# Routing groups, the pace of the second stage and the order of the tail in a fused attention and adapter kernel

## The chip, the core and the metric

The kernel runs on one core of a Trainium2 chip. The metric is the device time of one launch in microseconds, the median of three runs. One more execution was recorded by the hardware profiler; all rows below come from it. The engines are PE (TensorE, with PEld for its weight loads), DVE (VectorE), ACT (ScalarE), POOL (GpSimd) and SP, which here only issues DMAs. Each engine works through its own queue in order.

## The reference

Four batches of 12288 queries of 128 channels attend to a pooled key/value map, and the result runs through a mixture of rank-16 adapters, two out of eight per token.

```python
kv_pool = kv.reshape(B, H // 4, 4, W // 4, 4, C).mean(axis=(2, 4))    # 768 keys per batch
kv_flat = kv_pool.reshape(B, -1, C) @ w_sr                            # keys and values are one
a = softmax(q @ kv_flat.T / sqrt(C))
x = (a @ kv_flat).reshape(B * N, 128)
logits = x @ w_gate                                                   # 8 experts
w = softmax over the two largest logits, 0 elsewhere
out = x + sum over e of w[:, e] * (x @ A[e]) @ B[e]
```

## The kernel before

**Tiling.** The 49152 tokens are 96 chunks of 512 tokens (T), each as S = 4 sub-tiles of 128; NB = 24 chunks make a batch. The gate's logits come with the attention: `vx` holds, for each key, 128 value channels, 8 columns of value times w_gate, and a one, so that `acc` has 137 columns, the last being the softmax's denominator.

**First stage of a chunk.** `scores(k, r)`, r = 0..2: PE writes two 128x512 products into one of two `sg` buffers (pool ps_s) and ACT takes the exponential into `em`. `attend(k, s)`: PE sums 6 products of 137 columns for each sub-tile into `acc`, of which there is one buffer (ps_a). `normalize(k)`: DVE takes a reciprocal (L258) and one product of 128x544 (L263), which frees `acc`. `top(k)`: DVE sorts the 8 logits of each sub-tile (four MAX8, L281).

**Routing.** `route(k0)` makes the expert weights of a group of chunks at once: two differences, their sum `arg` and a comparison, then (`gates`) a tanh on ACT, a product and a sum into `gw`. The group sizes are `sizes` (L269), here 1, 1, 2, then 19 groups of 4, four of 2 and eight of 1. The operations of groups 0 and 1 run on DVE, the others on POOL (L287). For groups from chunk 4 on, the part from the tanh on is put into `later` and issued in the next slot, behind the exponential of `scores(k, 0)`; for the earlier ones it follows at once.

**Second stage of a chunk.** `transposes(kx, kh)`: PE turns the x of chunk kx and the gated hidden of chunk kh into one PSUM tile, and DVE copies both out (L333). `down(kx)`: four matmuls with A. `gate(kx)`: DVE multiplies by `gw` (L347). One slot later the gated hidden is transposed, another slot later `up` (four matmuls with B) and `finish` (DVE adds x, L360; SP stores). That is 16 matmuls of 128 columns a chunk. The tiles of `transposes`, `down` and `up` (and of the preparation and of `turn_q`) take turns on the two buffers of the pool ps_m: each new one waits until the tile two before it has been read.

**Slots.** The main loop runs over k = 4..95; I call one pass a slot. In slot k PE issues, in this order: `scores(k, 0)`; `transposes` of the entering chunk and of the one entered a slot ago; `scores(k, 1)`; `up` of the chunk entered two slots ago; a quarter of `attend` of the chunk in `att[k]`; `scores(k, 2)`; `down` of the entering chunk; the rest of `attend`. `att` has two chunks each in slots 6, 7 and 8, and chunk k-1 in slot k from slot 9 on. `normed[c]` is the slot in which chunk c is normalised and sorted; a group is routed in the slot of its last chunk. `enter` (L407) says which chunk enters the second stage in which slot: one a slot from slot 6 (chunk 0), and two at once in slots 85, 88 and 91, since 93 chunks must enter in 90 slots. The second of two is transposed, copied by DVE, taken `down` and gated at the end of the same slot, after the whole of `attend` (L477).

**Preparation of the next batch.** `prepare` gives 24 POOL additions (`sums`, 8 for each third h of the batch) and nine steps for PE and DVE (`rest`: keys, values and turn of each third). The additions come at the end of slots i = 10..20 of a batch (4, 3, 1, 0 a slot, three times), `rest` in slots i = 14, 15, 16, 18..23.

**Tail.** Behind slot 95, written out by hand (L568 on; K = 95): `up` and the finish of chunks K-4 and K-3, the whole second stage of K-2, K-1 and K. Chunk K is accumulated into an `sg` buffer (`o95`) and normalised in pieces: ACT takes two sub-tiles, DVE the logits and the other two (L589 to L596). Chunk K-1 is gated whole, ahead of chunk K's two halves (L618, L625, L626). The last operations are the additions of K-1, whole, and of K in halves (L643 to L645).

Of the kernel before, what the change touches and what calls it, by code (L numbers as in the profile page):

```python
# [10 lines left out]
FP32 = mybir.dt.float32  # L11
# [9 lines left out]
def kernel(  # L21
# [226 lines left out]
    def attend(k, s):  # L248
        b = k // NB
        if s == 0:  # L250
            acc[k] = ps_a.tile([P, S, 256], FP32, tag="acc", name="acc")
        o = acc[k][:, s, 0:VE]
        for j in range(J):
            mm(o, em[k][:, j, s * P:(s + 1) * P], vx[b][:, j], start=(j == 0), stop=(j == J - 1))
# [11 lines left out]

    sizes = [1, 1, 2] + [GC] * (NCHUNK // GC - 5) + [2] * 4 + [1] * 8  # L269
    first, size = {}, {}  # L270
    for n in sizes:
        k0 = len(first)
# [11 lines left out]

    def route(k0):
        n = size[k0] * S
        eng = nc.gpsimd if k0 > 1 else nc.vector  # L287
        lg = xg[k0].rearrange("p m s c -> p (m s) c")[:, 0:n, C:VC]
        so = srt[k0].rearrange("p m s e -> p (m s) e")[:, 0:n]

        def over(i):
            d = rpool.tile([P, GC * S, 8], FP32, tag=f"over{i}", name=f"over{i}")[:, 0:n]
            keep(eng.tensor_tensor(  # L293
                d, lg, so[:, :, i].unsqueeze(2).broadcast_to([P, n, 8]), op=ALU.subtract))
            return d

        arg, mask = over(0), over(1)
        keep(eng.tensor_tensor(arg, arg, mask, op=ALU.add))
        keep(eng.tensor_scalar(mask, mask, 0.0, None, op0=ALU.is_ge))


        def rest():
            gates(k0, n, eng, arg, mask)

        if k0 > 3:
            later.append(rest)
        else:
            rest()
# [6 lines left out]
        keep(eng.tensor_tensor(w[:, 0:n], w[:, 0:n], mask, op=ALU.add))  # L315
        gw[k0] = w

    def transposes(kx, kh):

        ps = mtile([P, 2, S, P], BF16, name="tt_ps")  # L320
        if kx is not None:
            xb = xn[kx].bitcast(U16)[:, :, 1::2].bitcast(BF16)
            for s in range(S):
                mm(ps[:, 0, s], xb[:, s, 0:C], id_bf, is_transpose=True,
                   start=(s == 0), stop=(s == S - 1))
        if kh is not None:
            for s in range(S):
                mm(ps[:, 1, s], hg[kh][:, s], id_bf, is_transpose=True,
                   start=(s == 0), stop=(s == S - 1))
        sb = run.tile([P, 2, S, P], BF16, tag="tts", name="tts")  # L330
        lo = 0 if kx is not None else 1
        hi = 2 if kh is not None else 1
        keep(nc.vector.tensor_copy(sb[:, lo:hi], ps[:, lo:hi]))  # L333
        if kx is not None:
            xT[kx] = sb[:, 0]
        if kh is not None:
            hgT[kh] = sb[:, 1]

    def down(k):
        hp[k] = mtile([P, S, P], name="h_ps")  # L340
        for s in range(S):
            mm(hp[k][:, s], xT[k][:, s], a_bf, start=(s == 0), stop=(s == S - 1))

    def gate(k):
        k0, m = first[k], k - first[k]
        hg[k] = run.tile([P, S, P], BF16, tag="hg", name="hg")
        keep(nc.vector.tensor_tensor(  # L347
            hg[k].rearrange("p s (e r) -> p (s e) r", e=E),
            hp[k].rearrange("p s (e r) -> p (s e) r", e=E),
            gw[k0][:, m * S:(m + 1) * S].rearrange("p s e -> p (s e)")  # L350
            .unsqueeze(2).broadcast_to([P, S * E, RK]), op=ALU.mult))
# [52 lines left out]
    for t, ks in att.items():  # L404
        for k in ks:
            normed[k] = t + 1 if k == ks[-1] else t
    enter = {}  # L407
    e = 0
    for k in range(NCHUNK):
        done = normed[first[k] + size[k] - 1]  # L410
        two = size[k] < GC and k % 4 == 0 and len(enter.get(e, [])) < 2
        e = max(e if two else e + 1, done + 1)
        enter.setdefault(e, []).append(k)

    sums, rest = [], []
    kh, ku = [], []
    for k in range(LA, NCHUNK):
        b, i = divmod(k, NB)
        ka = att.get(k, [])
        kx = enter.get(k, [])  # L420
        if k % GC == 0:
            g = k // GC
            if 2 <= g + 1 < B * NG:
                load_qT(g + 1)
            if 4 <= g + 2 < B * NG and g + 2 not in q_bf:
                cast_q(g + 2)
        if b + 1 < B:
            if i == 4:
                sums, rest = prepare(b + 1, nc.gpsimd)
            if 4 <= i < 16:  # L430
                h, j = divmod(i - 4, 4)
                load_kv(b + 1, h, j, None)

        def after_norm(kn):
            top(kn)
            if kn == first[kn] + size[kn] - 1:
                route(first[kn])

        kn = [n for n in att.get(k - 1, []) if normed[n] == k]
        if k == LA:  # L440
            for s in range(S):
                attend(0, s)
            ka = []
        scores(k, 0)
        while later:
            later.pop(0)()
        for n in kn:
            normalize(n)
        pairs = [(kx[j] if j < len(kx) else None, kh[j] if j < len(kh) else None)
                 for j in range(max(len(kx), len(kh)))]  # L450
        for x_, h_ in pairs[:1]:
            transposes(x_, h_)
        if k + 1 in range(GC + 1, 2 * GC):
            turn_q(1, (k + 1) % GC, nc.scalar)
        scores(k, 1)
        for u_ in ku:
            up(u_)
            finish(u_)
        for a_ in ka[:-1]:
            for s in range(S):  # L460
                attend(a_, s)
            normalize(a_)
            after_norm(a_)
        if ka and len(ka) == 1:
            attend(ka[0], 0)
        for n in kn:
            after_norm(n)
        scores(k, 2)
        for x_ in kx[:1]:
            down(x_)  # L470
            gate(x_)
        if rest and i in (14, 15, 16, 18, 19, 20, 21, 22, 23):
            rest.pop(0)()
        for a_ in ka[-1:]:
            for s in range(1 if len(ka) == 1 else 0, S):
                attend(a_, s)
        for x_, h_ in pairs[1:]:  # L477
            transposes(x_, h_)
        for x_ in kx[1:]:
            down(x_)  # L480
            gate(x_)
        ku = kh
        kh = kx
        if b + 1 < B and 10 <= i < 21:
            h, j = divmod(i - 10, 4)
            for _ in range((4, 3, 1, 0)[j]):
                sums[h].pop(0)()

    K = NCHUNK - 1
    assert kh == [K - 3] and ku == [K - 4], (kh, ku)  # L490
# [92 lines left out]
    gate_part(K - 2, 0, S)  # L583
    add_there(K - 4)

    ri = rpool.tile([P, S], FP32, tag="rinv", name="rinv")
    keep(nc.vector.reciprocal(ri, o95[:, :, VC]))
    xn[K] = xpool.tile([P, GC, S, VC], FP32, tag="xn", name="xn")[:, 0]
    for s in range(2):  # L589
        keep(nc.scalar.activation(xn[K][:, s, 0:C], o95[:, s, 0:C], AF.Copy, bias=0.0,  # L590
                                  scale=ri[:, s:s + 1]))
    lg = rpool.tile([P, S, E], FP32, tag="lg", name="lg")
    keep(nc.vector.tensor_tensor(lg, o95[:, :, C:VC], ri.unsqueeze(2).broadcast_to([P, S, E]),
                                 op=ALU.mult))
    keep(nc.vector.tensor_tensor(xn[K][:, 2:S, 0:C], o95[:, 2:S, 0:C],  # L595
                                 ri[:, 2:S].unsqueeze(2).broadcast_to([P, 2, C]), op=ALU.mult))  # L596
    tanhs()
    so = rpool.tile([P, S, 8], FP32, tag="so", name="so")
    for s in range(S):
# [15 lines left out]
    fetch(xT, K)  # L615
    th = rpool.tile([P, S, E], FP32, tag="th1", name="th1")
    keep(nc.scalar.activation(th, arg, AF.Tanh, bias=0.0, scale=0.5))
    gate_part(K - 1, 0, S)  # L618
    gw[K] = gpool.tile([P, S, E], FP32, tag="gw1", name="gw1")
    keep(nc.vector.scalar_tensor_tensor(gw[K], th, 1.0, mask, op0=ALU.add, op1=ALU.mult))  # L620
    down_into(K, ps_s)
    fetch(hgT, K - 2)
    carry(K - 3)
    add_there(K - 3)
    gate_part(K, 0, 2)  # L625
    gate_part(K, 2, S)  # L626
    up_into(K - 2, wide(bank(ps_s)))
    turn_h(K - 1, ps_m)
    fetch(hgT, K - 1)
    ps = bank(ps_m).bitcast(BF16).rearrange("p a b -> p (a b)")[:, 0:T].rearrange("p (s c) -> p s c", s=S)  # L630
    hgT[K] = run.tile([P, S, P], BF16, tag="tt1", name="tt1")
    for lo in (0, 2):
        for s in range(lo, lo + 2):
            mm(ps[:, s], hg[K][:, s], id_bf, is_transpose=True, start=(s == lo), stop=(s == lo + 1))
    keep(nc.scalar.copy(hgT[K][:, 0:2], ps[:, 0:2]))
    add_here(K - 2, 0, S, nc.sync)
    keep(nc.vector.tensor_copy(hgT[K][:, 2:S], ps[:, 2:S]))
    up_into(K - 1, bank(ps_m))
    dp[K] = wide(bank(ps_a))
    for lo in (0, 2):  # L640
        for s in range(lo, lo + 2):
            mm(dp[K][:, s], hgT[K][:, s], b_bf, start=(s == lo), stop=(s == lo + 1))
    add_here(K - 1, 0, S, nc.sync)  # L643
    add_here(K, 0, 2, nc.scalar)
    add_here(K, 2, S, nc.sync)  # L645


# [28 lines left out]
```

## Time and profile before

| what | value |
|---|---|
| median of 3 runs (lowest, highest) | 407.59 us (407.49, 407.65) |
| the profiled execution: time, span | 407.06 us, 405.0 us |
| mean granted TensorE clock | 0.992 |
| one exponential, 128x1024 (L246), x288 | 1023 ns, 278.9 us busy in all |
| normalise: reciprocal + product (L258, L263) | 181 + 724 ns |
| gate (L347), finish (L360), copy of two transposes (L333) | 690 ns each |
| copy of one transpose alone: DVE L333, ACT L514 | 422 ns, 585 ns |
| a routing operation on 32 columns: DVE, POOL (L293) | 188 ns, 245 ns |
| the same on 64 and on 128 columns on POOL (L293) | 306 ns, 422 ns |
| tanh on 32, 64, 128 columns (L312) | 232, 249, 302 ns |
| one POOL addition of the preparation, 128x512 (L171) | 1270 ns, x54 |
| a store: issue to landing | 3.6 us |

The span runs from the first to the last instruction; the launch adds some 2 us to it. A row of the profile's timeline gives the start, the busy time, the engine, the line, the operation with its output and inputs, the count, and in brackets how long the engine sat idle before it and whose work ended that. PE's matmuls overlap: one of 128 columns shows 219 ns, but eight follow each other in 0.45 us on the chain of waits. A table by stretches of time gives, for each engine, its busy time and the number of instructions in the stretch.

### The profile page before, as it was taken

To read this page: it belongs to the slowest core of one execution; us is meant where nothing else is said; L and a number is where in the kernel's file an instruction comes from. 1 tells how busy PE (TensorE), PEld (TensorE's weight loads), DVE (VectorE), ACT (ScalarE), POOL (GpSimd) and SP (SyncE) were. 2 spreads that over 40 slices of the span, in tenths; PEclk is the share of its full clock that TensorE was granted. 3 is DMA by queue.
4 is the path that set the end of the run, shared out by engine and by line. 5 is a ranking of instruction groups with operands and counts; after the bars stand their busy time and mean duration, and the time that the engine had idled before them with its cause. 6 is when DMAs were issued, how large, how long until landed. Compare 5 with 4: busy or idle time off the path is not lost.

```text
span 405.0 us, 11448 instructions
## 1 busy us (share of the span) xinstructions
PE 383.8 (95%) x4589; PEld 307.4 (76%) x4589; DVE 324.9 (80%) x950; ACT 292.2 (72%) x343; POOL 170.4 (42%) x289
## 2 busy tenths in 40 slices
PE   3898899999999999999999999999999999989893
PEld 3656778888888888888888888888888788777682
DVE  2543778888888888889888888889888888888885
ACT  2489468767678778767678778867678778667683
POOL 0010128778512318779411319779411313114342
PEclk9999999999999999999999999999999999999996
DMA  8997577994855999994844999996855765542213
GB/s 305 382 264 243 125 163 210 299 201 123 183 130 108 298 180 337 290 230 126 183 131 107 304 171 321 216 296 151 187 132 114 172 134 92 143 131 102 83 53 133
DMA packets 71318, 76.45 MB, mean 189 GB/s; under 512 B 49920, under 2 KB 50432, under 8 KB 70784
## 3 DMA queue, kind: packets, MB, share of 16 engines
q1 hardware_dynamic: 70128, 63.98, 55.3%
q0 software_dynamic: 704, 11.54, 16.8%
q8 instruction: 36, 0.59, 0.6%
q10 hardware_dynamic: 432, 0.20, 0.2%
q14 instruction: 18, 0.15, 0.1%
HBM read 50.53 MB, written 36.70 MB: 215 GB/s over the span
## 4 chain that ended last, share of the span: by engine, by line
PE 88%; DVE 5%; ACT 2%; DMA 1%; issue 1%; POOL 0%; DVEq 0%; ACTq 0%
PE acc L68 34%; PE sg L68 28%; PE tt_ps L68 9%; PE h_ps L68 5%; PE d_ps L68 5%; PE kpT_ps L68 2%; ACT em L246 2%; DVE xn L263 1%; DMA w_sr_sb<-in_w_sr_dram 1%; PE qT_ps L68 1%; PE v_ps L68 1%; DVE tts L333 1%; PE kfT_ps L68 1%; DVE hg L347 1%; DVE kvr L175 1%
## 5 line engine op out<-in xcount | busy, mean ns | idle before, releaser
L246 ACT ACTIVATE em<-sg 128x1024 f16<-128x1024 f32 x288 | 278.9, 1023 | 91.6 <-PE sg L68 91.4
L68 PE MATMUL sg<-qT,kfT 128*128 128x512 bf16 x576 | 170.9, 378 | 2.7 <-ACT em L246 2.2
L68 PE MATMUL acc<-vx,em 128*128 128x137 f16 x2280 | 171.6, 224 | 1.7 <-DVE xn L263 1.6
L68 PEld LDWEIGHTS <-em 128*128 128x128 f16 x2304 | 149.6, 98 | 4.0 <-DVE xn L263 2.2
L68 PEld LDWEIGHTS <-tts 128*128 128x128 bf16 x740 | 56.4, 98 | 45.8 <-DVE tts L333 2.1
L293 POOL TENSOR_TENSOR over<-xn,srt 128x128 f32<-128x128 f32 (+2 forms) x62 | 21.4, 363 | 157.2 <-DVE srt L281 157.2
L347 DVE TENSOR_TENSOR hg<-h_ps,gw 128x512 bf16<-128x512 f32 x93 | 64.2, 690 | 13.2 <-POOL gw L315 7.5
L263 DVE TENSOR_TENSOR xn<-acc,rinv 128x544 f32<-128x544 f32 x95 | 68.8, 724 | 3.3
L333 DVE COPY tts<-tt_ps 128x1024 bf16<-128x1024 bf16 (+1 forms) x96 | 64.4, 671 | 3.6 <-PE tt_ps L68 3.6
L171 POOL TENSOR_TENSOR kvr<-kvr 128x512 f32<-128x512 f32 x54 | 66.7, 1270 | 0.0
L360 DVE TENSOR_TENSOR osb<-d_ps,xn 128x512 f32<-128x512 f32 x91 | 62.5, 690 | 0.5 <-PE d_ps L68 0.5
L68 PEld LDWEIGHTS <-kfT 128*128 128x128 bf16 x576 | 45.9, 97 | 6.0 <-issue 3.7
L68 PEld LDWEIGHTS <-xn 128*128 128x128 bf16 x384 | 29.3, 98 | 21.9 <-DVE xn L595 0.5
L258 DVE RECIPROCAL rinv<-acc 128x4 f32<-128x4 f32 x95 | 17.2, 181 | 32.7 <-PE acc L68 31.5
L68 PE MATMUL h_ps<-a_bf,tts 128*128 128x128 bf16 x372 | 36.0, 219 | 1.6 <-DVE tts L333 1.6
L68 PE MATMUL d_ps<-b_bf,tts 128*128 128x128 bf16 x364 | 35.2, 219 | 1.3 <-DVE tts L333 1.3
L68 PE MATMUL tt_ps<-id_bf,xn 128*128 128x128 bf16 x372 | 35.9, 219 | 0.0
L68 PE MATMUL tt_ps<-id_bf,hg 128*128 128x128 bf16 x368 | 35.6, 219 | 0.3 <-DVE hg L347 0.3
L281 DVE MAX8 srt<-xn 128x8 f32<-128x8 f32 x380 | 34.2, 153 | 0.2
L314 POOL TENSOR_TENSOR gw<-th,over 128x128 f32<-128x128 f32 (+2 forms) x31 | 12.0, 387 | 37.1 <-ACT th L312 37.0
L68 PEld LDWEIGHTS <-hg 128*128 128x128 bf16 x384 | 25.4, 98 | 0.7 <-DVE hg L347 0.4
L169 POOL TENSOR_TENSOR kvr<-kvr 128x512 f32<-128x512 f32 (+1 forms) x18 | 18.1, 1004 | 0.9
(83 smaller groups left out, 175.4 us busy)
## 6 DMA issues: line engine op xcount, KB each, us to landing
out_dram<-osb SPq DMA_DIRECT2D x95, 256.0 KB, 3.6
kvr<-in_kv_dram SPq DMA_DIRECT2D x36, 512.0 KB, 6.3
qbf<-in_q_dram POOLq DMA_DIRECT2D x22, 512.0 KB, 6.3
kvr<-in_kv_dram SPq DMA_DIRECT2D x24, 256.0 KB, 4.9
qf<-in_q_dram SPq DMA_DIRECT2D x1, 1024.0 KB, 5.0
qf<-in_q_dram SPq DMA_DIRECT2D x4, 256.0 KB, 5.0
qT<-qbf SPq DMA_TRANSPOSE x22, 6.9
out_dram<-osb ACTq DMA_DIRECT2D x1, 128.0 KB, 3.2
```

The costliest lines, as they stand in the source:

```text
L68: return keep(nc.tensor.matmul(*a, **k))
L169: keep(adder.tensor_tensor(u, u, v, op=ALU.add))
L171: keep(adder.tensor_tensor(u[:, lo:hi], u[:, lo:hi], v[:, lo:hi], op=ALU.add))
L246: keep(nc.scalar.activation(em[k][:, 2 * r:2 * r + 2], ps, AF.Exp, bias=0.0, scale=scale))
L258: keep(nc.vector.reciprocal(ri, acc[k][:, :, VC]))
L263: keep(nc.vector.tensor_tensor(x, acc[k][:, :, 0:VC], ri.unsqueeze(2).broadcast_to([P, S, VC]), op=ALU.mult))
L281: keep(nc.vector.max(srt[k0][:, m, s], xn[k][:, s, C:VC]))
L293: keep(eng.tensor_tensor(d, lg, so[:, :, i].unsqueeze(2).broadcast_to([P, n, 8]), op=ALU.subtract))
L314: keep(eng.tensor_tensor(w[:, 0:n], th, mask, op=ALU.mult))
L333: keep(nc.vector.tensor_copy(sb[:, lo:hi], ps[:, lo:hi]))
L347: keep(nc.vector.tensor_tensor(hg[k].rearrange("p s (e r) -> p (s e) r", e=E), hp[k].rearrange("p s (e r) -> p (s e) r", e=E), gw[k0][:, m ...
L360: keep(nc.vector.tensor_tensor(osb, dp[k], xn[k][:, :, 0:C], op=ALU.add))
```

## The change

- **Groups.** `sizes` becomes four groups of 1, 34 of 2, 24 of 1. Chunks 0 to 3 are routed on DVE, the rest on POOL.
- **Entries.** `enter` is made from `ready`: the slot of a group's last normalisation, one more for chunks from 4 on and for chunk 2. One chunk a slot enters from slot 5 on (chunk 0), two in slots 73 (68, 69) and 75 (71, 72): 93 chunks in 91 slots. Chunk c up to 67 enters in slot c + 5 (before: c + 6 up to chunk 79), from chunk 72 on in slot c + 3.
- **The second of two.** Its transposes come before the last quarter of `attend`, and ACT copies them; its `down` follows `scores(k, 0)` of the next slot and its `gate` the first `transposes` there. Its hidden is transposed by the same late step two slots after it entered (again copied by ACT), and its `up` comes the slot after.
- **Preparation.** The additions come three at a time in even slots i = 6..20 (for the second batch in i = 8..20, four in 10, 14 and 18); the loads start at i = 0 from the third batch on; `rest` runs at i = 11, 12, 13, 17, 18, 19, 21, 22, 23 from the third batch on.
- **Tail.** Chunk K is normalised whole by DVE. Chunk K's halves are gated first, then K-1, in halves too. Both chunks go through transposes, ACT copies, `up` and additions in halves, K first.

```diff
-    sizes = [1, 1, 2] + [GC] * (NCHUNK // GC - 5) + [2] * 4 + [1] * 8
+    sizes = [1] * GC + [2] * (NB * (B - 1) // 2 - 2) + [1] * NB
...
-        eng = nc.gpsimd if k0 > 1 else nc.vector
+        eng = nc.gpsimd if k0 >= GC else nc.vector
...
-    def transposes(kx, kh):
+    def transposes(kx, kh, engine):
...
-        keep(nc.vector.tensor_copy(sb[:, lo:hi], ps[:, lo:hi]))
+        if engine is nc.scalar:
+            keep(nc.scalar.copy(sb[:, lo:hi], ps[:, lo:hi]))
+        else:
+            keep(nc.vector.tensor_copy(sb[:, lo:hi], ps[:, lo:hi]))
...
-    enter = {}
-    e = 0
-    for k in range(NCHUNK):
-        done = normed[first[k] + size[k] - 1]
-        two = size[k] < GC and k % 4 == 0 and len(enter.get(e, [])) < 2
-        e = max(e if two else e + 1, done + 1)
-        enter.setdefault(e, []).append(k)
+    ready = {k: normed[first[k] + size[k] - 1] + (k >= GC or k == 2) for k in range(NCHUNK)}
+    enter, t, left = {}, LA, list(range(NCHUNK - 3))
+    while left:
+        can = [k for k in left if ready[k] <= t]
+        enter[t] = can[:2] if t in (NB * (B - 1) + 1, NB * (B - 1) + 3) else can[:1]
+        left = [k for k in left if k not in enter[t]]
+        t += 1
...
-            if i == 4:
+            i0 = 4 if b == 0 else 0
+            if i == i0:
                 sums, rest = prepare(b + 1, nc.gpsimd)
-            if 4 <= i < 16:
-                h, j = divmod(i - 4, 4)
+                sums = sum(sums, [])
+            if i0 <= i < i0 + 12:
+                h, j = divmod(i - i0, 4)
                 load_kv(b + 1, h, j, None)
...
+        for x_ in kd:
+            down(x_)
         for n in kn:
             normalize(n)
...
-            transposes(x_, h_)
+            transposes(x_, h_, nc.vector)
+        for x_ in kd:
+            gate(x_)
...
+        kd = []
-        if rest and i in (14, 15, 16, 18, 19, 20, 21, 22, 23):
+        if rest and i in ((14, 15, 16, 18, 19, 20, 21, 22, 23) if b == 0 else (11, 12, 13, 17, 18, 19, 21, 22, 23)):
             rest.pop(0)()
         for a_ in ka[-1:]:
             for s in range(1 if len(ka) == 1 else 0, S):
+                if s == S - 1:
+                    for x_, h_ in pairs[1:]:
+                        transposes(x_, h_, nc.scalar)
+                        kd = [x_] if x_ is not None else []
                 attend(a_, s)
-        for x_, h_ in pairs[1:]:
-            transposes(x_, h_)
-        for x_ in kx[1:]:
-            down(x_)
-            gate(x_)
         ku = kh
-        kh = kx
-        if b + 1 < B and 10 <= i < 21:
-            h, j = divmod(i - 10, 4)
-            for _ in range((4, 3, 1, 0)[j]):
-                sums[h].pop(0)()
+        kh = kx[:1] + kdone
+        kdone = kd
+        if b + 1 < B and i % 2 == 0 and (8 if b == 0 else 6) <= i <= 20:
+            for _ in range(4 if b == 0 and i % 4 else 3):
+                sums.pop(0)()
...
-    for s in range(2):
-        keep(nc.scalar.activation(xn[K][:, s, 0:C], o95[:, s, 0:C], AF.Copy, bias=0.0,
-                                  scale=ri[:, s:s + 1]))
...
+    acc[K] = o95
+    normalize(K)
+    lg = xn[K][:, :, C:VC]
...
-    gate_part(K - 1, 0, S)
...
-    gate_part(K, 0, 2)
-    gate_part(K, 2, S)
+    halves = [(K, 0), (K, 2), (K - 1, 0), (K - 1, 2)]
+    for k, lo in halves:
+        gate_part(k, lo, lo + 2)
...
+    def half(ks, lo, lhs, rhs, transpose):
         for s in range(lo, lo + 2):
-            mm(ps[:, s], hg[K][:, s], id_bf, is_transpose=True, start=(s == lo), stop=(s == lo + 1))
...
+            kw = dict(is_transpose=True) if transpose else {}
+            mm(ks[:, s], lhs[:, s], rhs, start=(s == lo), stop=(s == lo + 1), **kw)
+
+    for k, lo in halves:
+        half(turned[k], lo, hg[k], id_bf, True)
+        keep(nc.scalar.copy(hgT[k][:, lo:lo + 2], turned[k][:, lo:lo + 2]))
+        if (k, lo) == (K, 2):
+            half(dp[K], 0, hgT[K], b_bf, False)
+            add_here(K - 2, 0, S, nc.sync)
+        elif k < K:
+            if lo == 0:
+                half(dp[K], 2, hgT[K], b_bf, False)
+                add_here(K, 0, 2, nc.sync)
+                add_here(K, 2, S, nc.sync)
+    dp[K - 1] = bank(ps_m)
+    half(dp[K - 1], 0, hgT[K - 1], b_bf, False)
+    add_here(K - 1, 0, 2, nc.scalar)
+    half(dp[K - 1], 2, hgT[K - 1], b_bf, False)
+    add_here(K - 1, 2, S, nc.sync)
```

More of the change, by code (lines that the diff above doesn't have):

```diff
@@ L406 @@
             normed[k] = t + 1 if k == ks[-1] else t
-    enter = {}
-    e = 0
-    for k in range(NCHUNK):
-        done = normed[first[k] + size[k] - 1]
-        two = size[k] < GC and k % 4 == 0 and len(enter.get(e, [])) < 2
-        e = max(e if two else e + 1, done + 1)
-        enter.setdefault(e, []).append(k)
+    ready = {k: normed[first[k] + size[k] - 1] + (k >= GC or k == 2) for k in range(NCHUNK)}
[5 more added lines that the diff above has]
+        t += 1
     sums, rest = [], []
-    kh, ku = [], []
+    kh, ku, kd, kdone = [], [], [], []
     for k in range(LA, NCHUNK):
@@ L584 @@
     add_there(K - 4)
-    ri = rpool.tile([P, S], FP32, tag="rinv", name="rinv")
-    keep(nc.vector.reciprocal(ri, o95[:, :, VC]))
-    xn[K] = xpool.tile([P, GC, S, VC], FP32, tag="xn", name="xn")[:, 0]
-    for s in range(2):
-        keep(nc.scalar.activation(xn[K][:, s, 0:C], o95[:, s, 0:C], AF.Copy, bias=0.0,
-                                  scale=ri[:, s:s + 1]))
[L592 to L596, printed above, removed]
+    acc[K] = o95
+    normalize(K)
+    lg = xn[K][:, :, C:VC]
     tanhs()
@@ L624 @@
     add_there(K - 3)
-    gate_part(K, 0, 2)
-    gate_part(K, 2, S)
+    halves = [(K, 0), (K, 2), (K - 1, 0), (K - 1, 2)]
+    for k, lo in halves:
+        gate_part(k, lo, lo + 2)
     up_into(K - 2, wide(bank(ps_s)))
[L628 to L632, printed above, removed]
-        for s in range(lo, lo + 2):
-            mm(ps[:, s], hg[K][:, s], id_bf, is_transpose=True, start=(s == lo), stop=(s == lo + 1))
[L635 to L645, printed above, removed]
+    dp[K] = wide(bank(ps_a))
+    turned = {k: bank(ps_m).bitcast(BF16).rearrange("p a b -> p (a b)")[:, 0:T]
+              .rearrange("p (s c) -> p s c", s=S) for k in (K - 1, K)}
+    for k in turned:
+        hgT[k] = run.tile([P, S, P], BF16, tag="tt1", name="tt1")
+    def half(ks, lo, lhs, rhs, transpose):
+        for s in range(lo, lo + 2):
+            kw = dict(is_transpose=True) if transpose else {}
[16 more added lines that the diff above has]
+    add_here(K - 1, 2, S, nc.sync)
 _INS = ['q', 'kv', 'w_sr', 'moe_w_gate', 'moe_A', 'moe_B']
```

## The prediction

> **What bounds the kernel now.** I read the page first, then a table by stretches of time, then the timeline of the stretches where PE is not full.
>
> ```profile
> PE 383.8 (95%) x4589; PEld 307.4 (76%) x4589; DVE 324.9 (80%) x950; ACT 292.2 (72%) x343; POOL 170.4 (42%) x289
> ...
> 37.83:43.55 5.72, 5.34 (x69) 4.44 (x67) 3.70 (x20) 3.44 (x6) 0.00 (x0) 1.00 1.18 329
> 43.55:49.68 6.13, 5.48 (x70) 4.17 (x68) 4.53 (x17) 2.79 (x3) 0.72 (x3) 1.00 0.25 81
> 49.68:55.95 6.27, 5.50 (x74) 4.50 (x72) 4.36 (x15) 4.02 (x5) 1.71 (x5) 1.00 0.56 95
> ...
> 56.00:344.00 288.00, 288.00 (x3572) 233.68 (x3570) 250.75 (x724) 221.59 (x248) 147.38 (x211) 1.00 0.79 194
> 344.00:388.00 44.00, 40.67 (x508) 32.46 (x507) 36.52 (x102) 30.08 (x37) 12.35 (x46) 1.00 0.36 109
> ```
>
> The first number pair of a stretch is its length and PE's busy time. From 56 to 344 us PE never rests: a slot takes 3.68 us, which is its matmuls end to end (six of 512 columns at 0.215, 24 of 137 columns in 1.49, 16 of 128 columns in 0.89, all from the chain of waits). Nothing can be won there, only lost. The change can win in slots 6 to 8 (37.83 to 55.95), in slots 85 to 94, where the three double entries lie, and in the tail. Slot 85's `scores(k, 0)` is at 343.71 and slot 95's at 384.33 + 3.68 = 388.01: ten slots in 44.30, 7.5 us more than 36.8, so 2.5 us for each double entry, of which 0.89 is matmuls.
>
> **Double entries.** Their stalls before:
>
> ```profile
> 348.30 0.40 PE L68 MATMUL h_ps<-a_bf,tts 128*128 128x128 bf16 x4 [0.52 <-DVE tts L333]
> 354.89 0.38 PE L68 MATMUL d_ps<-b_bf,tts 128*128 128x128 bf16 x4 [0.43 <-DVE tts L333]
> ```
>
> The second row is the one to learn from. The chunk's own hidden had been copied at 352.96 + 0.42; what ended at 354.83 is the copy of the next transposes, the tile two before this one in ps_m. So PE waits for the buffer. I carry that rule through the new order, with a normal slot's times from its start (from the slot at 340.04): `up` at 1.30, xn done at 1.13, copy to 1.76, `gate` 2.76 to 3.45.
>
> Slot 73 gains four matmuls, +0.22. In slot 74 the `down` of chunk 69 waits for ACT's copy (0.05), and takes a ps_m buffer that is freed only by `gate(69)`, which stands on DVE behind xn and the copy: 1.98 to 2.67. `up(67)` needs that very buffer, so it starts at 2.72 in place of 1.30: +1.42. Slot 75 has eight more matmuls, +0.44. Slot 76: ACT's copy of 1024 columns has no row; between twice the 512-column one (1.17) and an exponential of 1024 (1.02) I take 1.0; `down(72)` waits for it until 0.90, and `up(70)` again for the buffer of `gate(72)`, until 3.16; with a second `up` +2.1. Slots 77 and 78 add 0.22 and 0.52 (here `up(72)` waits for a copy, as in the second row). Sum 4.9 for two, 2.5 each as before; three become two: 4.9 - 7.5 = **-2.6**. Bounds: matmuls alone (1.8 for both), -5.7; 3.0 each, -1.5.
>
> **The start.** The third entry is not saved, it moves to slots 5 to 7, and the routing of chunks 2 and 3 moves from POOL to DVE. DVE is in the path there: `acc` has one buffer.
>
> ```profile
> 37.45 0.29 ACT L312 ACTIVATE th<-over 128x32 f32<-128x32 f32 x1
> 37.77 0.19 DVE L314 TENSOR_TENSOR gw<-th,over 128x32 f32<-128x32 f32 x1 [4.12 <-ACT th L312]
> 44.62 0.40 PE L68 MATMUL tt_ps<-id_bf,hg 128*128 128x128 bf16 x4 [0.25 <-DVE hg L347]
> ```
>
> Step by step, with the same row spacings. Slot 5 gets eight matmuls (0.45), partly under PE's waits for exponentials: slot 6 starts at 38.11, not 37.83. The first row does not move (ACT is full until there), so gw(0) is at 37.77 again; now `gate(0)` follows (0.33 later, 38.10) and only then reciprocal and xn of chunk 1 (+0.62, +0.21, +0.72: 39.65). Chunk 1 enters in the slot of its own normalisation, so PE, free at 38.54, stands until 39.71: 1.17. Then `attend(2)`, xn(2) ends at 43.66, `attend(3)` waits 0.55 (before 0.38). On DVE follow MAX8 of 2 (0.36), routing of 2 on 32 columns (difference to gw 0.85, as 42.70 to 43.55 in the trace, and 0.33 on), the same for chunk 1 (0.34 + 0.85 + 0.33), then `gate(1)`, 46.74 to 47.43. PE wants that hidden at 45.86 and gets it at 47.49: 1.63, where before it stood 0.25. Slot 8 adds 0.44 behind the routing of 3. Slot 9 starts at 58.68 in place of 55.95: **+2.7**, the extra 0.89 of matmuls in it.
>
> Then POOL:
>
> ```profile
> 61.69 0.45 POOL L314 TENSOR_TENSOR gw<-th,over 128x128 f32<-128x128 f32 x1 [0.99 <-ACT th L312]
> 62.22 0.46 POOL L315 TENSOR_TENSOR gw<-gw,over 128x128 f32<-128x128 f32 x1
> 62.64 7.42 POOL L171 TENSOR_TENSOR kvr<-kvr 128x512 f32<-128x512 f32 x6
> ```
>
> Before, additions start behind the gw of chunks 4 to 7. After, three of them end slot 8, and chunks 4 and 5 are routed in slot 8 with their gw in slot 9. POOL: differences from 57.86, comparison done at 59.3, three additions of 1.27 to 63.1, gw to 63.85. `gate(4)`, due in slot 9 near 61.4, is at 63.9; behind it on DVE wait reciprocal and xn of chunk 8. PE wants gate(4)'s hidden at 63.01 and gets it at 64.64: **+1.6**. With no such wait 0; with one addition more 2.9.
>
> By the Trainium skill (GPSIMD Engine Reference, Engine selection) element-wise work belongs on VectorE, with GpSimd about twice as slow. Rows agree in sign (188 against 245 ns); by the rule alone moving two routings (six operations each) is an estimated gain of 0.7 us at the rows' difference, by the queue above a loss.
>
> **The middle.** 34 pairs for 19 fours mean about 28 more tanhs at 0.23 to 0.25 us on ACT and six more POOL operations for each; ACT rests 0.7 us a slot, POOL is at 42%. Without these rests ACT's 7 us would show. The gates' waits for POOL (7.5 us of DVE over 19 groups of four) go; PE never saw them, since a slot leaves DVE 0.43 idle. One margin gets thin: the last addition before `keys(2)`. In slot 20 gw ends at 2.72, three additions (1.27, 1.27, 0.74) end at 6.1, 2.45 into slot 21, where PE wants them at 2.55; in the second batch the four of slot 18 push this 0.3 late. Taken **+0.2**; 0 to 1.
>
> **The tail.**
>
> ```profile
> 395.14 0.19 DVE L593 TENSOR_TENSOR lg<-sg,rinv 128x32 f32<-128x32 f32 x1 [0.69 <-ACT xn L590]
> 399.05 0.29 DVE L637 COPY tt<-tail_ps 128x256 bf16<-128x256 bf16 x1 [0.28 <-ACT tt L635]
> 399.95 0.75 DVE L547 TENSOR_TENSOR osb<-acc,xn 128x256 f32<-128x256 f32 x2
> ```
>
> Whole xn on DVE: 394.48 to 395.20, no wait for ACT; chunk K is turned at 395.49 (now past 395.8), fetched at 396.29 (396.68), and its gates start at 396.76 in place of 397.41. But four half gates at 0.37 then end at 398.29, against 398.16. If DVE then never waits (0.69 for K-2, four halves at 0.37) the last addition ends at 400.45, against 400.70: -0.25. The rows show DVE kept off a PSUM tile while ACT reads its other half; if PE is kept off in the same way, K-1's halves go one by one: transposes 398.35, ACT copy 398.68 to 399.05, transposes 399.10, copy to 399.79, `up` 399.84 to 400.08, additions to 401.07: +0.37. Granted clock is 0.5 from 399 on, so matmuls there may double (+0.3). I take **+0.3**, -0.3 to +0.7, by the nearer rows.
>
> The Trainium skill (PSUM — Partial Sum Buffer, PSUM bank collisions raise a hardware error) says that any two engines on one bank and partitions must be kept apart, whatever the columns; no row here shows it for PE against ACT. By it the tail is the +0.37 chain, without it -0.25.
>
> **Sum.** 2.7 + 1.6 - 2.6 + 0.2 + 0.3 = +2.2: span 405.0 to 407.2. The profiled execution is 407.06, the median 0.53 above it; I add to the median: **409.8 us**. A run of this kernel tells 0.2% (0.8 us) from no change.
>
> **Rivals.** (1) Faster: the split entries cost their matmuls alone. Place: `up` in slots 74 and 76; price 1.8 in place of 4.9. The gain begins when both together cost under 2.7; at the floor, 409.8 - 3.1 = 406.7. For it: matmuls are all that PE must do, and ACT has room for the copies. Against: the 354.89 row, which shows a wait for a buffer. 0.12. (2) No change to speak of: the gw of chunk 4 is not behind the additions (they wait for their loads, or POOL's order is another): 409.8 - 1.6 = 408.2. Against: POOL works in the order of the program in every row, and the first loads are issued at 33.36. 0.15. (3) Slower still: the additions come one late (1.27) for `keys(2)` in each of three batches: +3.6, 413.4. For it the margin of 0.1; against, PE stood for no preparation step from 56 to 344 and POOL idles before most routings. 0.06. The forecast has 0.67, with 408.4 to 411.4 as its own range. Rival 1 is faster but for 0.01 at its edge, rival 2 lies within 0.2%, the forecast and rival 3 are slower: 0.11, 0.16, 0.73. The range 407.1 to 411.5 leaves out most of rival 1 and rival 3.
>
> **What would show it.** Right: DVE's gw (L314) four times at the start, with PE's transposes of hg standing over 1 us in slots 6 to 8; slot 9 near 58.7; one `gate` waiting about 2 us for POOL near 62; `up` waiting for `hg` near slots 74 and 76, and no stall from slot 79 to 95; 3.68 us slots between. Wrong: slot 9 at 56 or 57; double slots at 0.9 each; a last addition that ends outside 12.4 to 13.4 us behind slot 95's start (before 400.70 - 388.01 = 12.7, forecast 13.0).

## The result and the profile after

The changed kernel takes as long as the one before, as far as can be told: the ratio of its time to the time before is 1.0014 (95% interval 0.999 to 1.0038). Its executions took 407.72 and 408.43 us, median 408.08 against 407.54 before; two more, of 414.77 and 416.24 us at a slightly lower mean granted clock, are left out, as is every execution over 1.5% above the fastest of its kernel in the times and ratios below. The profiled execution took 408.43 us with a span of 406.3, against 407.06 and 405.0 before: +1.3 in the span, where the medians differ by 0.5.

The first thing to look at is the page of the changed kernel, next to its line for `sg`.

```profile
PE 378.7 (93%) x4515; PEld 306.9 (76%) x4589; DVE 326.9 (80%) x957; ACT 296.9 (73%) x374; POOL 197.0 (48%) x445
...
L68 PE MATMUL sg<-qT,kfT 128*128 128x512 bf16 x502 | 155.0, 378 | 2.8 <-ACT em L246 1.8
```

PE seems less busy by 5 us, but 74 of the 576 matmuls of 512 columns have no record here. Its busy share says nothing this time; the starts of the slots do. I read them off the timeline, as the first `sg` of each slot:

| stretch | before, us | after, us | difference | forecast |
|---|---|---|---|---|
| start of the span to slot 6 | 37.83 | 38.39 | +0.56 | +0.28 |
| slots 6 to 8 | 18.12 | 21.17 | +3.05 | +2.45 |
| slot 9 | 3.68 | 3.68 | 0 | 0 |
| slot 10 | 3.68 | 5.21 | +1.53 | +1.6 |
| slots 11 to 72 | 236.25 | 236.75 | +0.50 | +0.2 |
| slots 73 to 94, both with their doubles | 88.45 | 84.95 | -3.50 | -2.6 |
| slot 95's start to the end of the span | 16.99 | 16.15 | -0.84 | +0.3 |

Of the first line, 0.27 is there before slot 4 begins (the first load takes 5.47 us for 5.13). This is not the change's doing: in the ten profiles of this case slot 4 begins anywhere between 30.9 and 32.3 us. The same stretches in a table by windows of the changed kernel: slot 10; slots 73 and 74; 75 and 76; 77 and 78; the tail (length, then the busy time and count of PE, PEld, DVE, ACT and POOL; granted clock; DMA share; GB/s).

```profile
63.24:68.45 5.21, 3.86 (x50) 2.97 (x48) 3.57 (x10) 3.33 (x5) 4.80 (x11) 1.00 0.44 138
305.20:313.56 8.36, 7.92 (x102) 6.30 (x101) 6.93 (x19) 6.59 (x9) 2.59 (x9) 1.00 0.25 83
313.56:323.18 9.62, 8.49 (x110) 6.80 (x110) 7.53 (x20) 7.07 (x9) 3.48 (x14) 1.00 0.57 137
323.18:331.27 8.09, 7.86 (x101) 6.42 (x101) 6.92 (x19) 6.63 (x9) 2.97 (x12) 1.00 0.48 160
390.15:406.30 16.15, 10.12 (x132) 8.01 (x130) 10.66 (x35) 8.53 (x18) 6.13 (x17) 0.87 0.29 106
```

Six slots from 73 to 78 take 26.07 in place of six times 3.68 = 22.08: 4.0 us for two doubles. From slot 79 on every slot takes 3.68.

**The start**, from the timeline of the changed kernel:

```profile
38.05 0.19 DVE L314 TENSOR_TENSOR gw<-th,over 128x32 f32<-128x32 f32 x1 [1.00 <-ACT th L312]
40.16 0.40 PE L68 MATMUL tt_ps<-id_bf,xn 128*128 128x128 bf16 x4 [1.18 <-DVE xn L263]
48.26 0.40 PE L68 MATMUL tt_ps<-id_bf,hg 128*128 128x128 bf16 x4 [1.75 <-DVE hg L350]
54.47 0.40 PE L68 MATMUL tt_ps<-id_bf,hg 128*128 128x128 bf16 x4 [0.26 <-DVE hg L350]
```

PE stands 1.18 us for the x of chunk 1 in slot 6, 1.75 for the hidden of chunk 1 in slot 7, 0.26 for that of chunk 2 in slot 8: the three places of the forecast (1.17, 1.63, 0.44).

**Slots 8 to 10**, same view:

```profile
60.24 3.71 POOL L171 TENSOR_TENSOR kvr<-kvr 128x512 f32<-128x512 f32 x3
63.93 0.31 POOL L314 TENSOR_TENSOR gw<-th,over 128x64 f32<-128x64 f32 x1
64.66 0.69 DVE L350 TENSOR_TENSOR hg<-h_ps,gw 128x512 bf16<-128x512 f32 x1 [2.40 <-POOL gw L315]
65.41 0.40 PE L68 MATMUL tt_ps<-id_bf,hg 128*128 128x128 bf16 x4 [1.35 <-DVE hg L350]
```

Read downwards it is one chain: three additions on POOL, gw behind them though its tanh had long been done (61.17 + 0.25), the gate behind gw, PE behind the gate.

**The doubles**, slots 74 and 76:

```profile
310.45 0.69 DVE L336 COPY tts<-tt_ps 128x1024 bf16<-128x1024 bf16 x1 [0.20 <-PE tt_ps L68]
311.06 0.68 DVE L350 TENSOR_TENSOR hg<-h_ps,gw 128x512 bf16<-128x512 f32 x1
311.19 0.38 PE L68 MATMUL d_ps<-b_bf,tts 128*128 128x128 bf16 x4 [0.35 <-DVE tts L336]
...
318.58 0.40 PE L68 MATMUL h_ps<-a_bf,tts 128*128 128x128 bf16 x4 [0.52 <-ACT tts L334]
320.21 0.38 PE L68 MATMUL d_ps<-b_bf,tts 128*128 128x128 bf16 x4 [0.35 <-DVE tts L336]
320.81 0.38 PE L68 MATMUL d_ps<-b_bf,tts 128*128 128x128 bf16 x4 [0.21 <-DVE hg L350]
```

The `up` at 311.19 starts when the copy is done (311.14), and while the gate of the split chunk still runs, to 311.74. So it took the buffer that the transposes had used, not the one of the `down` two tiles before it. In slot 76 the first `up` again follows the copy and only the second the gate.

**The tail**, timeline of the changed kernel, and the landing of its half stores next to the half store before (issues: count, size, us to landing; the first two lines are of the changed kernel, the third is of the kernel before):

```profile
400.25 0.27 PE L68 MATMUL tail_ps<-id_bf,hg 128*128 128x128 bf16 x2 [0.52 <-ACT tt L642]
402.45 0.37 PE L68 MATMUL tail_ps<-b_bf,tt 128*128 128x128 bf16 x2 [0.81 <-DVE osb L556]
402.86 0.42 DVE L556 TENSOR_TENSOR osb<-tail_ps,xn 128x256 f32<-128x256 f32 x1 [0.46 <-PE tail_ps L68]
```

```profile
out_dram<-osb SPq DMA_DIRECT2D x3, 128.0 KB, 2.3
out_dram<-osb ACTq DMA_DIRECT2D x1, 128.0 KB, 2.4
```

```profile
out_dram<-osb ACTq DMA_DIRECT2D x1, 128.0 KB, 3.2
```

PE does not write one half of a PSUM tile while ACT or DVE still reads the other: it stands 0.52 and 0.81 us. The last addition ends at 403.28, 13.13 behind slot 95's start, later than the 12.69 before. But from there to the end of the span are 3.0 us, where the kernel before needed 4.3. In all ten profiles the span ends 1.1 to 1.3 us behind the landing of the last store, so it is the landing that moved: 15.06 us behind slot 95's start, 15.84 before.

### The profile page after: what moved, and what is told of

Read it like the earlier page. It is cut to its first block, busy times and chain, and to the rows that moved or that the text cites. A ratio compares the mean times of both kernels' runs of the same rounds, so it can differ in the third digit from the quotient of the medians.

```text
span 406.3 us, 11617 instructions
## 1 busy us (share of the span) xinstructions
PE 378.7 (93%) x4515; PEld 306.9 (76%) x4589; DVE 326.9 (80%) x957; ACT 296.9 (73%) x374; POOL 197.0 (48%) x445
## 4 chain that ended last, share of the span: by engine, by line
PE 82%; DVE 6%; DMA 6%; ACT 2%; issue 2%; POOL 1%; DVEq 0%; POOLq 0%; ACTq 0%
PE acc L68 32%; PE sg L68 23%; PE tt_ps L68 10%; PE h_ps L68 6%; PE d_ps L68 5%; DMA qT<-qbf 4%; PE kpT_ps L68 2%; ACT em L246 1%; DMA w_sr_sb<-in_w_sr_dram 1%; DVE rinv L258 1%; PE qT_ps L68 1%; DVE xn L263 1%; PE v_ps L68 1%; POOL kvr L171 1%; DVE hg L350 1%
## 5 line engine op out<-in xcount | busy, mean ns | idle before, releaser
L68 PE MATMUL sg<-qT,kfT 128*128 128x512 bf16 x502 | 155.0, 378 | 2.8 <-ACT em L246 1.8
L293 POOL TENSOR_TENSOR over<-xn,srt 128x64 f32<-128x64 f32 (+1 forms) x114 | 29.7, 282 | 86.1 <-DVE srt L281 85.9
L336 DVE COPY tts<-tt_ps 128x1024 bf16<-128x1024 bf16 (+1 forms) x91 | 62.6, 688 | 4.9 <-PE tt_ps L68 4.9
L314 POOL TENSOR_TENSOR gw<-th,over 128x64 f32<-128x64 f32 (+1 forms) x57 | 16.6, 291 | 76.5 <-ACT th L312 76.4
L299 POOL TENSOR_SCALAR over<-over 128x64 f32<-128x64 f32 (+1 forms) x57 | 19.0, 333 | 5.2
```

The costliest lines, as they stand in the source:

```text
L68: return keep(nc.tensor.matmul(*a, **k))
L293: keep(eng.tensor_tensor(d, lg, so[:, :, i].unsqueeze(2).broadcast_to([P, n, 8]), op=ALU.subtract))
L314: keep(eng.tensor_tensor(w[:, 0:n], th, mask, op=ALU.mult))
```

## The experiments

Times are medians of the executions. The kernel before is run beside them: 407.56 us beside the two edits of the start one by one, the new tail alone and the split alone, 407.70 beside the other four runs.

**Additions moved by a slot.** Is it POOL's queue that makes slot 10 long?

```diff
-        if b + 1 < B and i % 2 == 0 and (8 if b == 0 else 6) <= i <= 20:
-            for _ in range(4 if b == 0 and i % 4 else 3):
+        adds = {9: 3, 10: 2, 12: 4, 14: 4, 16: 4, 18: 4, 20: 3} if b == 0 else dict.fromkeys(range(6, 21, 2), 3)
+        if b + 1 < B:
+            for _ in range(adds.get(i, 0)):
                 sums.pop(0)()
```

> The changed kernel with the first three POOL additions of the second batch moved from the end of slot 8 to the end of slot 9 (then 2, 4, 4, 4, 4, 3 in slots 10 to 20). Theory, POOL's queue: gate(4) waited 2.40 us for gw behind these additions, and slot 10 took 5.21 us; now the wait is gone, slot 10 takes 3.68 and the span is 1.5 us shorter than 406.3: 404.8. Rival, DVE is late there anyway: slot 10 stays above 4.5 and the span within 0.5 of 406.3.

406.18 us, ratio to the kernel before 0.9961 (0.9948 to 0.9975); span of its profile 403.5. Slot 10 takes 3.68. The rows of POOL and of the gate there:

```profile
60.87 0.32 POOL L314 TENSOR_TENSOR gw<-th,over 128x64 f32<-128x64 f32 x1 [1.29 <-ACT th L312]
61.27 0.32 POOL L315 TENSOR_TENSOR gw<-gw,over 128x64 f32<-128x64 f32 x1
61.70 0.69 DVE L350 TENSOR_TENSOR hg<-h_ps,gw 128x512 bf16<-128x512 f32 x1
63.03 3.73 POOL L171 TENSOR_TENSOR kvr<-kvr 128x512 f32<-128x512 f32 x3
```

The gate no longer waits. POOL's order was the whole cost of slot 10; the rival is out.

**Routing of chunks 2 and 3 on POOL.**

```diff
-        eng = nc.gpsimd if k0 >= GC else nc.vector
+        eng = nc.gpsimd if k0 > 1 else nc.vector
```

> The changed kernel with chunks 2 and 3 routed on POOL, not DVE; entries as in the changed kernel. Theory, DVE's queue is the path at the start: two routings of about 1.2 us leave it, PE's wait for the hidden of chunk 1 (1.75 us) falls to about 0.6 and the one for chunk 2 may grow, slots 6 to 8 (21.2 us together) lose 1 to 2 us, span 404.5 to 405.3. Rival, the early entries alone cost the start (chunk 1 turned in the slot of its own normalisation): slots 6 to 8 lose under 0.4 us.

406.90 us, 0.9981 (0.9972 to 0.9991). Slots 6 to 8 take 7.30, 6.55 and 6.05, together 19.90 in place of 21.17: -1.27, as the first theory had it. The wait for the hidden of chunk 1 is now

```profile
47.75 0.40 PE L68 MATMUL tt_ps<-id_bf,hg 128*128 128x128 bf16 x4 [0.58 <-DVE hg L350]
```

What is left, 19.90 against 18.12, is by the rows the early entry: 1.8 us, of which eight more matmuls in these three slots are 0.45 and PE's wait for a chunk that is turned in the slot of its own normalisation is 1.18 (slot 6 stays at 7.30). No run takes the early entry alone back.

**Both edits of the start together.**

> The changed kernel with both edits of the start: the second batch's additions from slot 9, and chunks 2 and 3 routed on POOL. Alone they gave 406.1 to 406.4 and 406.2 to 407.6 where the changed kernel gave 407.7 and 408.4. Theory, two separate waits that add up: slot 10 takes 3.68, slots 6 to 8 19.9, 405.0 to 405.4. Rival, one queue in both (POOL, now with two routings more, is late again): no better than the first edit alone, 406.1.

405.52 us, 0.9969 (0.9943 to 0.9995). Slot 10 takes 3.68 and slots 6 to 8 take 7.30, 6.54 and 6.05: the two waits are separate, as the first theory says. The time is less clear than the slots: seven executions lie between 404.88 and 405.85, one at 406.75 and two near 410. The profiled one is among the latter; what it lost is told at the end. With such a spread the ratio is no test of 0.2%, so that the two gains add up is read from the slots.

**The new tail on the kernel before.** The tail's code (from the first `turn_x(K - 2, ps_m)` on) is put under the loop of the kernel before, unchanged.

> The kernel before with the new tail alone. From slot 95's start to the end of the span the kernel before takes 16.99 us, the changed one 16.15. Theory, the new tail's last additions end 0.4 us later but its last store is of 128 KB and lands sooner: 16.15 here too, span 404.2, time 0.8 us under the kernel before. Rival, the tail's gain comes from what the late slots left behind: within 0.3 us of the kernel before.

407.48 us, 0.9997 (0.9988 to 1.0006): nothing that can be told. In its profile the stretch takes 16.78 us, 0.2 under before: the last addition ends 0.56 later (13.25), the end of the span follows 3.5 us behind it in place of 4.3. The expected 16.15 did not come; both parts of the theory are there in sign, but they nearly cancel. The half stores of this run, issued at the same places of the tail as in the changed kernel, land later than the 2.3 us there:

```profile
out_dram<-osb SPq DMA_DIRECT2D x3, 128.0 KB, 2.8
```

So the tail's code alone does not set how soon they land.

**Double entries split, on the kernel before.** `kd`, `kdone`, ACT's copy and the later `down` and `gate`, word for word as in the change; entries stay in slots 85, 88 and 91.

```diff
+        for x_ in kd:
+            down(x_)
         for n in kn:
             normalize(n)
...
+        for x_ in kd:
+            gate(x_)
...
             for s in range(1 if len(ka) == 1 else 0, S):
+                if s == S - 1:
+                    for x_, h_ in pairs[1:]:
+                        transposes(x_, h_, nc.scalar)
+                        kd = [x_] if x_ is not None else []
                 attend(a_, s)
-        for x_, h_ in pairs[1:]:
-            transposes(x_, h_)
-        for x_ in kx[1:]:
-            down(x_)
-            gate(x_)
```

> The kernel before with its three double entries (slots 85, 88, 91) split over two slots and copied by ACT, as the change does; nothing else. Before, each costs 2.5 us over its slots. Theory: up waits only for the first copy of its slot, each costs 0.22 + 0.78 + 0.22 + 0.51 = 1.7 us as the rows of slots 73 to 78 of the changed kernel give, three cost 5.2 in place of 7.5, span 402.7. Rival, as in the prediction: up waits for the gate of the split chunk, 2.5 us each, span 405.0.

405.65 us, 0.9948 (0.9935 to 0.9962): -1.9. Slot 85's start to slot 95's takes 42.15 in place of 44.30, so a split double costs (42.15 - 36.80) / 3 = 1.78 and an unsplit one 2.5. The first double's rows repeat the order seen in the changed kernel:

```profile
349.47 0.69 DVE L336 COPY tts<-tt_ps 128x1024 bf16<-128x1024 bf16 x1 [0.21 <-PE tt_ps L68]
350.08 0.68 DVE L350 TENSOR_TENSOR hg<-h_ps,gw 128x512 bf16<-128x512 f32 x1
350.22 0.38 PE L68 MATMUL d_ps<-b_bf,tts 128*128 128x128 bf16 x4 [0.35 <-DVE tts L336]
```

`up` waits 0.35 us for the copy, not for the gate. The prediction's 2.5 is refuted; the 1.7 worked out from the changed kernel's rows is near. The three splits gain 2.15 us in these slots and the time 1.9, since the stretch behind them takes 0.2 longer (17.23 us for 16.99).

**Split doubles and the new tail on the kernel before.**

> The kernel before with the split double entries and the new tail, its own routing groups and preparation. Split alone gave 405.65 us, the new tail alone nothing that could be told (407.48 against 407.56). Theory, the tail gains nothing by itself: 405.2 to 405.8, slot 95's start to the end of the span 16.6 to 17.2 us. Rival, it gains the 0.8 us seen in the changed kernel once the late slots are single: 404.8, 16.15 us.

404.55 us, 0.9923 (0.9911 to 0.9935), all five executions between 404.29 and 405.21: faster than both kernels. The tail's stretch takes 16.41 us, against 17.23 in the profile with the split alone, and the time is 1.1 below that one, so here the tail does gain, though not all the way to 16.15. My first theory, that it gains nothing, is wrong at this place; alone it gained nothing to speak of. The difference lies between the last addition and the end (3.3 against 4.7 us; 3.5 against 4.3 without the split). Why the new tail's stores land sooner behind split doubles than behind unsplit ones, and the old tail's later (4.7 against 4.3), stays open.

**One store of 256 KB at the end**, on the changed kernel:

```diff
-    add_here(K - 1, 0, 2, nc.scalar)
+    osb = opool.tile([P, S, C], FP32, tag="osb", name="osb")
+    keep(nc.vector.tensor_tensor(osb[:, 0:2], dp[K - 1][:, 0:2], xn[K - 1][:, 0:2, 0:C], op=ALU.add))
     half(dp[K - 1], 2, hgT[K - 1], b_bf, False)
-    add_here(K - 1, 2, S, nc.sync)
+    keep(nc.vector.tensor_tensor(osb[:, 2:S], dp[K - 1][:, 2:S], xn[K - 1][:, 2:S, 0:C], op=ALU.add))
+    keep(nc.sync.dma_start(dest(K - 1), osb))
```

> The changed kernel with chunk K-1's two halves written by one store of 256 KB behind the second addition, in place of two of 128 KB on two queues. Theory, the tail's end is set by how much the last stores still have to move: from the end of the last addition to the end of the span 3.0 us become 3.5 to 4.0, time +0.5 to +1. Rival, a store's landing does not depend on its size here: 2.9 to 3.2.

408.08 us, 1.0015 (1.0006 to 1.0025), against 1.0014 for the changed kernel. The last addition ends at the same 13.13 behind slot 95's start, the end follows 3.3 us later in place of 3.0. The direction is that of the first theory, the size under half of what it asked for, and the time does not show it: inconclusive. What is still to be moved at the end explains a part of the 1.3 us at most.

**All batches prepared as the second.** `i0 = 4` for all, additions in even slots from 8, `rest` from 14.

> The changed kernel with all batches prepared in the slots in which the change prepares the second: loads in i = 4 to 15, additions in even slots from 8, keys, values and turn from 14. Theory, the earlier loads delay the transposing DMA of qT (median to landing 8.3 us in the changed kernel, 6.9 before, one of 16.9 that PE waited 0.37 us for): median near 7, no wait of PE for it, span 0.4 to 0.6 us under 406.3, and all executions within 0.5% of each other. Rival, the DMA is late because of the stores and the start: median stays above 8 and some executions again take over 414 us.

407.83 us, 1.0003 (0.9995 to 1.0012), eleven executions between 407.27 and 408.35, span 406.2: the 0.4 to 0.6 us did not come. The qT loads still take 8.1 us in the median (8.3 in the changed kernel), so the theory that the earlier loads delay qT is refuted. Why qT lands later than before (6.9) stays open. Slots 11 to 72 take 236.13, against 236.25 before: the middle costs nothing when PE does not stand for a load.

## Why the prediction was wrong

It said 409.8, slower by more than can be mistaken for no change; measured is 408.1, no difference that can be told. Its causes at the start were right, two of its terms were not: the double entries and the tail. That 408.1 lies beside rival 2's 408.2 says nothing for rival 2: its condition was not met, gw did stand behind the additions.

- **What bounds the kernel**: right. Slots without a double or preparation take 3.68 us after, too; more tanhs and more POOL work are not seen.
- **The start, +2.7**: the mechanism is right at all three places, and the experiment that took two routings off DVE confirmed whose queue it was (-1.27). The term is 3.3: after the routings of chunks 0 and 1, from gw to the gate 0.52 and 0.53 us pass (38.05 to 38.57, 46.98 to 47.51), not the 0.33 that I took from the row before. That is 0.4 of the 0.6 us.
- **The additions ahead of gw, +1.6**: right, 1.53, and shown by moving them alone.
- **The double entries, -2.6**: the sign is right, the size wrong: -3.5. The step that failed is "takes a ps_m buffer that is freed only by `gate(69)`", with its +1.42 and +2.1; measured are +0.78 (slot 74, 8.36 - 3.90 - 3.68) and 1.81 (slot 76, 317.69 to 323.18). I read the 354.89 row as "the tile two before this one". The rows of both split kernels show that a new tile gets the buffer whose last read stands earlier in the program: the copy, not the gate. In the kernel before the two readings name the same buffer, so that row could not tell them apart. The prediction's rival, matmuls alone, is not right either: a split double costs 2.0 in the changed kernel and 1.8 in the split alone, not 0.9.
- **The middle, +0.2**: +0.5 in the profiled execution, 0.42 of it PE's wait at 270.29 for one qT load that took 16.9 us. In four other profiles (additions moved, routing on POOL, one last store, all batches as the second) these slots take 236.1 to 236.2, so in general the middle costs nothing. The preparation's last addition cost nothing.
- **The tail, +0.3**: the term is mis-sized in a part I had not priced at all. The chain to the last addition was right: 13.13, forecast 13.0, and PE is kept off a half-read tile, which the prediction had left between two values. As the Trainium skill has it (PSUM — Partial Sum Buffer, PSUM bank collisions raise a hardware error), two engines are kept apart on one bank even at different columns; the 0.52 and 0.81 us rows agree. The step that failed here is that I took what follows the last addition as unchanged, without a reason: it fell from 4.3 to 3.0 us, since the last store landed sooner. What makes it land sooner is not shown.

The late first load (0.27), the start up to slot 9 (3.3) and slot 10 (1.5) cost 5.1 and the middle 0.5; the doubles (3.5) and the tail (0.8) gave back 4.3: +1.3 in the profile. The late first load and the middle are of this execution; without them 0.5 is left, which is what the medians show.

## What to carry to other kernels

Part of a large change can be worth more than all of it: here two edits of the second half, put on the old schedule, give -0.8%, while the early entries, the routing on DVE and the earlier additions gave it back at the start. The early entries did not pay even with the routing on POOL: they save one split double (42.15 - 36.80 = 5.35 us for three, 26.07 - 22.08 = 3.99 for two, so 1.4), and slots 4 to 8 take 26.68 us with them, 24.62 before. When work is moved forward in a queue, look for what the next slot's consumer has queued behind it: three additions of 1.27 us cost 1.5 us only because a 0.3 us product stood behind them. And find out by which rule a pool hands out its buffers before costing a wait on one; a row in which two rules agree is no evidence for either.

## What was not expected of the hardware

In the profiled execution with both edits of the start, PE stops in the middle of four equal transposes, with nothing of the program to wait for that the profile shows, and 1.2 us after it goes on the granted clock is halved (timeline, then two windows):

```profile
157.58 0.22 PE L68 MATMUL tt_ps<-id_bf,hg 128*128 128x128 bf16 x1
160.88 0.33 PE L68 MATMUL tt_ps<-id_bf,hg 128*128 128x128 bf16 x3 [3.08 <-issue]
```

```profile
150.00:153.00 3.00, 3.00 (x42) 2.53 (x40) 2.88 (x8) 2.74 (x3) 2.87 (x4) 1.00 1.62 67
...
162.00:164.00 2.00, 2.00 (x14) 1.38 (x12) 1.20 (x6) 1.52 (x2) 0.89 (x4) 0.51 0.94 365
```

The slot takes 8.76 us; the same slot with the first edit alone takes 3.93. Of the 4.8 us more, the pause is 3.1; the clock, 0.5 from 162.05 to 165.47, accounts for the remaining 1.7. In the stretch before, the DMA engines' share is 1.62 while only 67 GB/s move; a transposing qT load issued at 145.10 was then on its way and landed 17.7 us later. The DMA packets show one thing more: of the 36 loads of instructions of 16 KB each (queue q8), the one that starts at 156.08 takes 3.30 us, the longest in all ten profiles; the median here is 1.02. That PE stood for these instructions fits, but no run changes this load, so the cause is not shown.
